# A gated linear attention in front of two MLP blocks: each 128-token unit's attention done in two halves of 64 tokens

## The chip, the core and the metric

The kernel runs on one core of a Trainium2 chip. The metric is device time in microseconds (us) of one execution, taken as the median of several runs. A second source is one execution recorded by the hardware profiler, whose trace gives start and duration of the instructions on each engine: PE (TensorE matmuls), PEld (TensorE weight loads), DVE (VectorE), ACT (ScalarE), POOL (GpSimd), SP (SyncE, which issues the DMAs).

## The reference

```python
# q, k, v, f_logit: (4, 8, 768, 48) float32
f = 1.0 / (1.0 + np.exp(-f_logit))
for t in range(S):
    state = f[:, :, t, :, None] * state + np.einsum('bhd,bhe->bhde', k[:, :, t], v[:, :, t])
    y[:, :, t] = np.einsum('bhd,bhde->bhe', q[:, :, t], state)
x = y as (4, 768, 384)
xn = (x - mean) / np.sqrt(var + 1e-06) * g_ln
x = x + np.maximum(xn @ w_ch1, 0.0) @ w_ch2                      # (384 -> 1536 -> 384)
h = np.maximum(x.transpose(0, 2, 1) @ w_tok1, 0.0) @ w_tok2      # over the 768 tokens, 256 wide
u = x + h.transpose(0, 2, 1)
out = u + np.maximum(u @ w2_ch1, 0.0) @ w2_ch2
```

## The kernel before, in words

**Units.** The tokens are cut into NU = 24 units of C = 128 tokens, one batch each: unit n is chunk c = n // 4 of batch b = n % 4. So units 0 to 3 start from an empty state (c = 0), and units 20 to 23 are the last of their batch (`last`) and need not hand a state on.

**Attention of a unit** (function `attention(n)`). The gates become a running sum along the tokens (`scan`); K is multiplied by exp(sum) (`km`) and Q by exp(-sum) (`qm`), after which the recurrence is a masked product without gates. The 8 heads lie as 4 pairs p, with the two heads r of a pair on partitions 0 to 47 and 64 to 111. The items that run on TensorE are:

- `kp`: 4 transposes of K, evicted by ACT as `kt`;
- `sc`: scores K·Q, for each of 8 heads in two halves of the key tokens, 48 rows by 64 columns of the array, with all 128 query tokens moving. DVE multiplies them with the upper-triangular mask `upper` and writes A (`A0`, `A1`, one for each r);
- `y`: the carried part state·Q (48 rows, only if c > 0), and then the inner part V·A (all 128 rows), summed in the PSUM tiles `yT`;
- `st`: the new part of the state, V·kt (128 rows, 48 moving columns), which `ste` adds to `state[b]` and `std` decays on POOL;
- `yt`: 4 transposes of the result, then `lna`, `lnc` make the layer norm's input, and `tp`: 3 transposes, split by `ah`, `al` into the two parts that the MLP reads.

These are float32 matmuls, and each appears in the trace as two instructions (16 calls of `sc` are 32 instructions).

**MLP.** The weights arrive as 64-bit numbers; `convert` turns each tile of 128x384 into a high and a low float32r part: `.ld` a DMA, `.a`, `.b`, `.c` on DVE, `.h` on ACT, `.l` on DVE or POOL. The first block's MLP takes three units in a step (8 steps); a piece is 9 matmuls of 128x384 (`mm1`, line 492, and `mm2`, line 522). The second block (lines 549, 570, 730, 754) has the same weights' place and follows.

**Order of the work.** Each engine works in the order in which the program emits its instructions. Two mechanisms set it. Up to time slot J = 77 a list written out by hand, `ORDER`, names every item; there `n.sc` is unit n's item, `w3.a` a step of weight tile 3, `m0.4` a piece of MLP step 0, `m0.o20` one of its second product, and `+k` puts k filler matmuls (`busy`, line 439, bf16, 224 columns of zeros, result unused) ahead of the item. After slot 77 the items are sorted by their slot numbers: unit n has s0 = M0 - LEAD + 8(n - 3), its items stand at s0 plus the offset in the table at the end of `attention`, and the MLP puts one piece at every whole slot. `POOL` lists the items that run on GpSimd instead of VectorE; from unit `NV` on, `clamp`, `km` and `qm` all do.

[...]

Of the kernel before, what the change touches and what calls it, by code (L numbers as in the profile page):

```python
# [155 lines left out]
def main_path(ctx, tc, q_t, k_t, f_t, v_n, g_rep, w1, w2, wt1, wt2, w3, w4, out, x1_d, f_d):  # L156
# [11 lines left out]
    upper = const.tile([128, 128], F32, name="upper")  # L168
# [4 lines left out]
    rs = const.tile([128, NU], F32, name="rs")  # L173
    zeros = const.tile([128, 224], BF16, name="zeros")
# [58 lines left out]
    vp = at.enter_context(tc.tile_pool(name="vp", bufs=2))  # L233
# [4 lines left out]
    state = [s1.tile([P2, NP * D], F32, name=f"state{b}") for b in range(B)]  # L238
# [4 lines left out]
    def attention(n):  # L243
# [75 lines left out]

        def scores(z=0):  # L320
            t["sc"] = [scp.tile([128, NP, 128], F32, tag="sc", name="sc") for _ in range(2)]
            busy(t["sc"][0].rearrange("p a c -> p (a c)"), z)
            for p in range(NP):
                for r in range(2):
                    for s in (slice(0, 64), slice(64, 128)):
                        nc.tensor.matmul(t["sc"][r][s, p], t["K"][rows(r), p, s], t["Q"][rows(r), p, :])  # L326

        def scores_e(g):
            a = s2.tile([128, NP, 128], F32, tag=f"A{g}", name=f"A{g}")
            t["A", g] = a  # L330
            nc.vector.tensor_tensor(
                a, t["sc"][g], upper.rearrange("p (o c) -> p o c", o=1).to_broadcast([128, NP, 128]),
                op=ALU.mult)

        def outp(z=0):


            t["yT"] = [atp.tile([128, NP, 128], F32, tag="at", name="yT") for _ in range(2)]
            busy(t["yT"][0].rearrange("p a c -> p (a c)"), z)
            heads = [(p, r, slice(64 * (p % 2), 64 * (p % 2) + (D if p % 2 else 64)))  # L340
                     for p in range(NP) for r in range(2)]
            if c:
# [3 lines left out]
            for p, r, o in sorted(heads, key=lambda x: x[1]):
                h = head(p, r)
                nc.tensor.matmul(t["yT"][r][o, p // 2], t["V"][:, D * h:D * h + o.stop - o.start],  # L348
                                 t["A", r][:, p, :], start=(c == 0 and p < 2), stop=(p > 1))

        def outp_e(r):
            if not r:
                t["ys"] = s1.tile([P2, 2, 2, 128], F32, tag="ys", name="ys")
            nc.scalar.activation(out=t["ys"][:, r], in_=t["yT"][r][:P2, :2], func=AF.Copy)
# [8 lines left out]

        def stat():
            ps = t["st"] = t["yT"][0].rearrange("p a c -> p (a c)")[:, 256:256 + NP * D]
            kt, v = t["kt"], t["V"]
            for p in range(NP):
                for r in range(2):
                    h = head(p, r)
                    w = D if r else 64  # L370
                    nc.tensor.matmul(ps[64 * r:64 * r + w, D * p:D * p + D],  # L371
                                     kt[:, P2 * p + 64 * r:P2 * p + 64 * r + w], v[:, D * h:D * h + D])

        def stat_d():
            s = state[b].rearrange("p (a c) -> p a c", a=NP)
            nc.gpsimd.tensor_tensor(s, s, t["dec"].to_broadcast([P2, NP, D]), op=ALU.mult)

        def stat_e():
            new = t["st"][:P2]
            if c:  # L380
                nc.vector.tensor_tensor(state[b], new, state[b], op=ALU.add)
            else:
                nc.scalar.activation(out=state[b], in_=new, func=AF.Copy)
# [36 lines left out]
        for d, add, f, name in (  # L420
# [12 lines left out]
            if f:  # L433
                add(s0 + d, f, f"{n}.{name}")
# [176 lines left out]
    def start():  # L611
# [11 lines left out]
        for s in state:  # L623
            nc.gpsimd.memset(s, 0.0)
# [429 lines left out]
```

## Time and profile before

| what | value |
|---|---|
| median of 3 runs | 785.78 us (785.74, 785.78, 786.79) |
| span of the profiled execution, first to last instruction | 784.8 us |
| PE busy | 774.3 us, 99% of the span |
| DVE, ACT, POOL busy | 409.8, 325.8, 209.2 us |
| granted TensorE clock | full in all but the last slices |
| chain of work that ended last | PE 92%, DMA 4%, DVE 2% |

The span is 1.0 us below the median of the runs. Busy time of PE is the union of its matmuls, whose recorded durations overlap; how fast matmuls really follow each other is read from the starts of neighbouring groups in the timeline.

### The profile page before, as it was taken

The page shows a single profiled execution, that of the slowest core. Times are in us where ns is not written, and L with a number is a line of the kernel's source. Part 1 is how long each engine was busy: PE and PEld are TensorE (multiplying, and loading weights), DVE is VectorE, ACT ScalarE, POOL GpSimd, SP SyncE. Part 2 cuts the span into 40 slices and gives each one's busy share as a digit, 9 for nine tenths or more (in the row PEclk, how much of TensorE's full clock was granted, in tenths as well). Part 3 has the DMA queues.
Part 4 walks back from the last instruction along what each step waited for, and adds up shares of the span by engine and source line. Part 5 has one row for each costly group of instructions (what it writes and reads, how often), then busy time and mean ns, then how long its engine had stood idle before and what let it go on. Part 6 is the DMA issues. An engine that isn't in the chain of part 4 may idle for free.

```text
span 784.8 us, 14459 instructions
## 1 busy us (share of the span) xinstructions
PE 774.3 (99%) x5785; PEld 727.9 (93%) x5785; DVE 409.8 (52%) x742; ACT 325.8 (42%) x817; POOL 209.2 (27%) x270
## 2 busy tenths in 40 slices
PE   8899999999999999999999999999999999999997
PEld 7799999999999999999999898899899899899886
DVE  6789996564655556554363444434434444344421
ACT  6773552443534435342252544334424344334210
POOL 3642344333433323430014441211111111112000
PEclk9999999999999999999999999999999999999999
DMA  9743553444434445441343632324333342323101
GB/s 252 229 130 107 168 154 101 149 127 156 148 113 142 130 150 153 138 136 51 101 120 95 192 115 84 110 81 132 112 81 91 111 141 74 109 81 104 38 2 44
DMA packets 48604, 93.24 MB, mean 119 GB/s; under 512 B 5520, under 2 KB 26128, under 8 KB 48528
## 3 DMA queue, kind: packets, MB, share of 16 engines
q1 hardware_dynamic: 48528, 92.23, 39.3%
q8 instruction: 47, 0.77, 0.4%
q14 instruction: 29, 0.24, 0.1%
HBM read 76.48 MB, written 15.73 MB: 117 GB/s over the span
## 4 chain that ended last, share of the span: by engine, by line
PE 92%; DMA 4%; DVE 2%; ACT 1%; issue 0%; POOL 0%; SPq 0%; POOLq 0%
PE mo L570 19%; PE mm L549 19%; PE mo L522 19%; PE mm L492 18%; PE rt L730 3%; PE ht L754 3%; PE sc L326 3%; PE yT L348 2%; PE tp L445 2%; DMA firstv<-in_w 1%; PE yT L344 1%; DMA sg<-in_w 1%; PE yT L371 1%; PE y L362 1%; DMA first<-in_k_t 1%; PE kp L310 1%
## 5 line engine op out<-in xcount | busy, mean ns | idle before, releaser
L492 PE MATMUL mm<-xt,w1h 128*128 128x384 f32 x576 | 150.0, 341 | 0.1
L807 POOL TENSOR_TENSOR cs<-cs 128x384 f32<-128x384 f32 x56 | 46.6, 832 | 226.5 <-DVE cs L804 155.9
L492 PEld LDWEIGHTS mm<-xt,w1h 128*128 128x128 f32 x576 | 102.1, 188 | 1.1 <-DVE xt L478 0.3
L522 PE MATMUL mo<-w2h,hh 128*128 128x384 f32 x288 | 100.2, 348 | 0.0
L560 DVE SCALAR_TENSOR_TENSOR hl<-mm,hh 128x512 fp32r<-128x512 f32 x72 | 49.7, 691 | 92.4 <-ACT hh L556 92.4
L570 PE MATMUL mo<-w2h,hh 128*128 128x384 f32 x288 | 97.5, 338 | 0.0
L492 PE MATMUL mm<-xt,w1l 128*128 128x384 f32 x288 | 96.6, 336 | 0.1
L522 PE MATMUL mo<-w2h,hl 128*128 128x384 f32 x288 | 96.6, 335 | 0.0
L570 PE MATMUL mo<-w2h,hl 128*128 128x384 f32 x288 | 96.5, 335 | 0.0
L522 PE MATMUL mo<-w2l,hh 128*128 128x384 f32 x288 | 96.3, 335 | 0.0
L570 PE MATMUL mo<-w2l,hh 128*128 128x384 f32 x288 | 96.3, 334 | 0.0
L556 ACT ACTIVATE hh<-mm 128x512 fp32r<-128x512 f32 x72 | 43.0, 598 | 121.2 <-PE mm L549 121.2
L507 ACT ACTIVATE hh<-mm 128x384 fp32r<-128x384 f32 x96 | 46.9, 489 | 70.0 <-PE mm L492 70.0
L511 DVE SCALAR_TENSOR_TENSOR hl<-mm,hh 128x384 fp32r<-128x384 f32 x96 | 52.9, 554 | 41.5 <-ACT hh L507 41.2
L549 PE MATMUL mm<-xt,w1h 128*128 128x512 f32 x216 | 67.1, 392 | 0.0
L600 DVE TENSOR_TENSOR xr<-mo,xr 128x384 f32<-128x384 f32 x48 | 26.7, 556 | 74.2 <-PE mo L570 74.2
L522 PEld LDWEIGHTS mo<-w2h,hh 128*128 128x128 f32 x288 | 54.1, 188 | 1.3 <-issue 0.9
L570 PEld LDWEIGHTS mo<-w2h,hh 128*128 128x128 f32 x288 | 54.1, 188 | 0.5
L570 PEld LDWEIGHTS mo<-w2l,hh 128*128 128x128 f32 x288 | 54.1, 188 | 0.4
L492 PEld LDWEIGHTS mm<-xt,w1l 128*128 128x128 f32 x288 | 54.1, 188 | 0.4 <-DVE w1l L227 0.4
L522 PEld LDWEIGHTS mo<-w2l,hh 128*128 128x128 f32 x288 | 54.2, 188 | 0.0
L570 PEld LDWEIGHTS mo<-w2h,hl 128*128 128x128 f32 x288 | 54.0, 188 | 0.0
(157 smaller groups left out, 1514.0 us busy)
## 6 DMA issues: line engine op xcount, KB each, us to landing
cs<-in_w SPq DMA_DIRECT2D x48, 384.0 KB, 3.2
sg<-in_w SPq DMA_DIRECT2D x44, 384.0 KB, 3.7
f_d<-cu SPq DMA_DIRECT2D x32, 192.0 KB, 2.0
wf<-f_d SPq DMA_DIRECT2D x32, 192.0 KB, 2.6
F<-in_f_t SPq DMA_DIRECT2D x21, 224.0 KB, 2.8
T<-in_k_t SPq DMA_DIRECT2D x21, 224.0 KB, 2.9
T<-in_q_t SPq DMA_DIRECT2D x21, 224.0 KB, 3.4
x_d<-x SPq DMA_DIRECT2D x24, 192.0 KB, 1.9
```

The source lines that it names most:

```text
L326: nc.tensor.matmul(t["sc"][r][s, p], t["K"][rows(r), p, s], t["Q"][rows(r), p, :])
L492: nc.tensor.matmul(ps, w[:, f, k, :], x[:, k, :], start=(i == 0), stop=(i == 8))
L507: nc.scalar.activation(out=hid(f)[0], in_=t[f], func=AF.Relu)
L511: nc.vector.scalar_tensor_tensor(hl, t[f], 0.0, hh.bitcast(F32), op0=ALU.max, op1=ALU.subtract)
L522: nc.tensor.matmul(ps, x, w[:, f, :], start=(f == lo and i == 0), stop=(f == hi and i == 2))
L549: nc.tensor.matmul(ps, w[:, f, k, :], x[:, k, :], start=(i == 0), stop=(i == 8))
L556: nc.scalar.activation(out=hid(f)[0], in_=t[f], func=AF.Relu)
L560: nc.vector.scalar_tensor_tensor(hl, t[f], 0.0, hh.bitcast(F32), op0=ALU.max, op1=ALU.subtract)
L570: nc.tensor.matmul(ps, x, w[:, f, :], start=(f == lo and i == 0), stop=(f == hi and i == 2))
L600: nc.vector.tensor_tensor(x, ps, x, op=ALU.add)
L730: nc.tensor.matmul(t["r"][j][:, :DM], w[:, s, js], t[x, s], start=(s == 0 and i == 0), stop=(s == NCH - 1 and i == 2))
L807: nc.gpsimd.tensor_tensor(t["u"], t["u"], t["h"], op=ALU.subtract)
```

## The change

The unit's 128 tokens become two halves of HC = 64. Scores are computed only for query and key tokens of the same half, so the half block of the score matrix that the mask set to zero is left out, and the block between the halves is replaced by the state after the first half (`mid`).

- `sc`: the same 16 calls, but 64 moving columns instead of 128; the mask is 64 wide, and `A0`, `A1` have 256 columns instead of 512.
- `st` stands right behind `sc` and gives the state's new part of each half separately: 16 calls of 64 rows instead of 8 of 128. `stm` (new, DVE) makes `mid` = old state + first half's part; `ste` makes the new state from `mid` in a second buffer. Last units need `mid` too, so they now have `kp`, `kt`, the first half of `st`, and `stm`.
- `y` is the carried part of the first half and the inner part for r = 0; `z` (new) is the inner part for r = 1 and the carried part of the second half from `mid`, also in units with c = 0. All use 64 rows and 64 moving columns. Between them stands `yw`: DVE sets one element (`done`) once `y`'s last matmul has ended, and `z`'s first matmul waits for that, since from there on the other half of the array's rows writes a PSUM bank.
- The evictions `yc0`, `yc1` keep their sizes; K's transposes get one buffer for `kt` instead of two, V one more.
- `ORDER`, `POOL`, `A`, LEAD (3 to 7), NV (9 to 12) and the offsets of the slots are new. The initial memsets of `state` go, and two small POOL copies make the narrower mask.

```diff
-P = dict(A=[10, 13, 19, 25, 33, 41, 52, 59, 67], M0=29, LEAD=3, WS=9, ... NV=9, ...)
+P = dict(A=[7, 10, 16, 22, 30, 38, 46, 54, 62], M0=29, LEAD=7, WS=9, ... NV=12, ...)
-POOL: w0.l 3.clamp w1.l 3.km 4.clamp w5.l w12.l w13.l 5.clamp w14.l w16.l w6.l 6.qm w18.l 7.km 8.clamp w20.l
-    w22.l 8.qm 9.clamp 9.qm
+POOL: 3.clamp 0.km 4.clamp 1.km 1.qm 2.km 3.km 3.qm w12.l 5.clamp 4.km 4.qm w1.l w2.l w0.l 6.clamp 5.qm 5.km w4.l
+    w3.l w5.l 6.qm 6.km w13.l w14.l 7.clamp w17.l w15.l 7.qm 9.clamp w18.l 8.km w6.l 8.qm w11.l w7.l 10.clamp w8.l
+    9.qm 9.km 10.qm w19.l w20.l w22.l w21.l w23.l 11.km 11.qm
...
         def scores(z=0):
-            t["sc"] = [scp.tile([128, NP, 128], F32, tag="sc", name="sc") for _ in range(2)]
+            t["sc"] = [scp.tile([128, 512], F32, tag="sc", name="sc") for _ in range(2)]
             for p in range(NP):
                 for r in range(2):
-                    for s in (slice(0, 64), slice(64, 128)):
-                        nc.tensor.matmul(t["sc"][r][s, p], t["K"][rows(r), p, s], t["Q"][rows(r), p, :])
+                    for i in range(2):
+                        nc.tensor.matmul(t["sc"][r][half(i), HC * p:HC * p + HC], t["K"][rows(r), p, half(i)],
+                                         t["Q"][rows(r), p, half(i)])
+        def stat():
+            for p in range(NP):
+                for i in range(1 if last else 2):
+                    for r in range(2):
+                        h, w = head(p, r), width(r)
+                        o = NP * HC + D * p
+                        nc.tensor.matmul(t["sc"][i][64 * r:64 * r + w, o:o + D],
+                                         t["kt"][half(i), P2 * p + 64 * r:P2 * p + 64 * r + w],
+                                         t["V"][half(i), D * h:D * h + D])
+        def stat_m():
+            t["S"] = old(), s1.tile([P2, NP * D], F32, tag="mid", name="mid")
+            if c:
+                nc.vector.tensor_tensor(t["S"][1], new(0), old(), op=ALU.add)
+            else:
+                nc.vector.tensor_copy(t["S"][1], new(0))
+        def carried(i):
+            s = t["S"][1] if i else old()
+            for p in range(NP):
+                for r in range(2):
+                    o = slice(64 * (p % 2), 64 * (p % 2) + width(p % 2))
+                    nc.tensor.matmul(t["yT"][r ^ i][o, r, p // 2], s[rows(r), D * p:D * p + width(p % 2)],
+                                     t["Q"][rows(r), p, half(i)], ...)
+        def inner(r):
+            for p in range(NP):
+                for i in range(2):
+                    h = head(p, r)
+                    o = slice(64 * (p % 2), 64 * (p % 2) + width(p % 2))
+                    nc.tensor.matmul(t["yT"][r ^ i][o, r, p // 2], t["V"][half(i), D * h:D * h + width(p % 2)],
+                                     t["A", r][half(i), p], ...)
         def outp(z=0):
+            t["yT"] = [atp.tile([128, 2, 2, HC], F32, tag="at", name="yT") for _ in range(2)]
             if c:
-                for p, r, o in heads: ... state[b][rows(r), ...], t["Q"][rows(r), p, :]
-            for p, r, o in sorted(heads, key=lambda x: x[1]): ... t["V"][:, ...], t["A", r][:, p, :]
+                carried(0)
+            inner(0)
+            t["half"] = nc.cur_bb.bb.instructions[-1]
+        def outp_w():
+            nc.vector.memset(done, 0.0)
+            t["done"] = nc.cur_bb.bb.instructions[-1]
+            follow(t["done"], t["half"])
+        def outp2():
+            block = nc.cur_bb.bb
+            z = len(block.instructions)
+            inner(1)
+            carried(1)
+            follow(block.instructions[z], t["done"])
...
-                (-8.5, sl.e, pre_km, "km"), (-9, sl.e, pre_tot, "tot"), (-3, sl.p, None if last else ktrans, "kp"),
-                (-2, sl.e, None if last else ktrans_e, "kt"), (-6.1, sl.p, scores, "sc"),
-                (-5, sl.e, ... "A0"), (-5, sl.e, ... "A1"), (2, sl.p, outp, "y"), (3, sl.e, ... "yc0"), (3, sl.e, ... "yc1"),
-                (4, sl.p, outp_t, "yt"), (5, sl.e, ln_a, "lna"), (2, sl.p, None if last else stat, "st"), ...
-                (7, sl.p, trans, "tp"),
+                (-8.5, sl.e, pre_km, "km"), (-9, sl.e, pre_tot, "tot"), (-7, sl.p, ktrans, "kp"),
+                (-6, sl.e, ktrans_e, "kt"), (-4.7, sl.p, scores, "sc"), (-4.7, sl.p, stat, "st"),
+                (-4, sl.e, ... "A0"), (-4, sl.e, ... "A1"), (-3.5, sl.e, stat_m, "stm"), (-3.5, sl.e, ... "ste"),
+                (-2.5, sl.e, ... "std"), (3, sl.p, outp, "y"), (3.05, sl.e, outp_w, "yw"), (3.2, sl.p, outp2, "z"),
+                (4, sl.e, ... "yc0"), (4, sl.e, ... "yc1"), (5, sl.p, outp_t, "yt"), ... (11.1, sl.p, trans, "tp"),
```

The two lists `ORDER` are too long to stand here. These are their items for TensorE alone, in order, the attention's and the fillers (`m` stands for one or more MLP pieces in between):

```
before: 0.kp+17 0.sc 1.kp 0.y+8 0.st 1.sc 0.yt 2.kp+8 0.tp+6 1.y 1.st 2.sc 1.yt 3.kp+4 3.sc 2.y 1.tp 2.st 2.yt+11 4.kp
 4.sc+6 2.tp 3.y 3.st m 3.yt 4.y 4.st m 3.tp 4.yt 5.kp 5.sc 4.tp+4 5.y+6 5.st m 5.yt m+5 5.tp m+10 (m pieces, one +3) 6.kp
 m 6.sc m 7.kp m 6.y 6.st m 6.yt m 8.kp 6.tp 7.sc m 8.sc 7.y m 9.kp m 7.st 9.sc 8.y 8.st m 7.yt m 8.yt m 7.tp m 8.tp m
 10.sc 9.y 9.st m
after: 0.kp+14 0.sc 0.st 0.y+3 1.kp+11 0.z 1.sc 0.yt 1.st 2.kp 1.y 2.sc 0.tp 1.z 2.st 3.kp 2.y 1.yt 2.z 3.sc 3.st 2.yt
 3.y+3 1.tp 3.z 4.kp+3 2.tp 4.sc 3.yt 4.st m 4.y m 4.z m 3.tp 5.kp 5.sc 4.yt 5.st m 5.y m 5.z m 6.kp 6.sc 5.yt m 4.tp
 6.st 5.tp m 6.y m 7.kp m 6.z m 7.sc m 7.st m 6.yt m 7.y m 8.kp 8.sc 7.z m 8.st m 8.y m 7.yt 8.z m 9.kp 9.sc m 9.st m
 8.yt m 9.y 10.kp m 9.z 6.tp 10.sc 8.tp m 10.st 7.tp 9.yt m
```

In the list before, the first weight loads come in the order w5, w0, w14, w15, w13, w4, w3, w1, w2; in the one after, w12, w1, w2, w0, w3, w4, w5, w17, w13, w14.

## Rows read from the trace of the kernel before

**Rows 1.** The profile's page: busy us of each engine (share of the span), instructions.

```profile
PE 774.3 (99%) x5785; PEld 727.9 (93%) x5785; DVE 409.8 (52%) x742; ACT 325.8 (42%) x817; POOL 209.2 (27%) x270
```

**Rows 2.** Waits of TensorE in the whole span: total us, times, longest.

```profile
PE sc L326 <- DVE A L331: 1.7, 1, 1.7
...
PE yT L348 <- DVE A L331: 0.2, 1, 0.2
```

**Rows 3.** Busy us of each engine by stretch (PE, PEld, DVE, ACT, POOL), granted clock, DMA share.

```profile
10.70:35.00 24.30, 21.72 (x373) 18.25 (x373) 19.62 (x33) 17.59 (x45) 13.88 (x18) 1.00 0.92 279
...
10.70:52.70 42.00, 39.28 (x587) 33.99 (x587) 35.72 (x66) 32.08 (x86) 22.21 (x29) 1.00 0.72 214
...
140.70:191.10 50.40, 50.40 (x491) 48.66 (x490) 28.44 (x52) 20.95 (x52) 18.22 (x24) 1.00 0.45 140
```

**Rows 4.** Timeline of TensorE, one unit: start us, us, engine, line, tiles, shapes, count.

```profile
303.69 0.34 PE L492 MATMUL mm<-xt,w1l 128*128 128x384 f32 x1
303.95 1.10 PE L326 MATMUL sc<-T 48*64 48x128 f32 x32
304.88 0.62 PE L344 MATMUL yT<-T,state 48*64 48x128 f32 x16
305.42 1.09 PE L348 MATMUL yT<-A,V 128*64 128x128 f32 x16
306.34 0.62 PE L371 MATMUL yT<-V,kt 128*48 128x48 f32 x16
306.89 0.44 PE L492 MATMUL mm<-xt,w1h 128*128 128x384 f32 x1
...
310.14 0.55 PE L362 MATMUL y<-ident,ys 112*128 112x112 f32 x4
```

**Rows 5.** Timeline of TensorE elsewhere: MLP alone, `sc` alone, `kp`, a last unit.

```profile
65.56 0.33 PE L522 MATMUL mo<-w2h,hh 128*128 128x384 f32 x1
65.73 0.33 PE L522 MATMUL mo<-w2l,hh 128*128 128x384 f32 x1
...
83.23 1.10 PE L326 MATMUL sc<-T 48*64 48x128 f32 x32
84.26 0.44 PE L522 MATMUL mo<-w2h,hh 128*128 128x384 f32 x1
...
295.31 0.55 PE L310 MATMUL kp<-ident,T 112*128 112x112 f32 x4
295.62 0.60 PE L492 MATMUL mm<-xt,w1h 128*128 128x384 f32 x2
...
336.26 1.10 PE L326 MATMUL sc<-T 48*64 48x128 f32 x32
...
338.75 0.44 PE L522 MATMUL mo<-w2h,hh 128*128 128x384 f32 x1
```

**Rows 6.** Timeline of all engines, cut to 303.90 to 303.98 us.

```profile
303.95 0.34 PE L326 MATMUL sc<-T 48*64 48x128 f32 x4
```

**Rows 7.** Timeline of TensorE at the start: fillers (L439) and what followed.

```profile
18.24 0.60 PE L310 MATMUL kp<-ident,first 112*128 112x112 f32 x4 [0.40 <-DVE first L296]
...
27.41 1.21 PE L439 MATMUL y<-zeros 128*128 128x224 bf16 x11 [0.25 <-ACT ys L354]
28.46 0.55 PE L362 MATMUL y<-ident,ys 112*128 112x112 f32 x4
```

**Rows 8.** Groups of DVE and POOL instructions by line, start of the span.

```profile
L331 DVE TENSOR_TENSOR A<-sc,upper 128x512 f32<-128x512 f32 x12 | 8.0, 684 | 0.7 <-PE sc L326 0.7
L299 DVE TENSOR_TENSOR T<-T,eq 112x512 f32<-112x512 f32 x3 | 2.1, 688 | 0.0
L299 POOL TENSOR_TENSOR T<-T,eq 112x512 f32<-112x512 f32 x5 | 8.3, 1662 | 7.3 <-ACT eq L293 7.3
L296 POOL TENSOR_TENSOR T<-T,ek 112x512 f32<-112x512 f32 x5 | 6.6, 1321 | 2.8 <-DMA T<-in_k_t 1.8 <-ACT ek L289 1.0
L227 POOL TENSOR_TENSOR w1l<-cu,w1h 128x384 fp32r<-128x384 f32 x4 | 4.2, 1052 | 3.6 <-ACT w1h L226 3.6
```

More of the change, by code (lines that the diff above doesn't have):

```diff
@@ L173, in main_path @@
     rs = const.tile([128, NU], F32, name="rs")
+    done = const.tile([1, 1], F32, name="done")
     zeros = const.tile([128, 224], BF16, name="zeros")
@@ L237, in main_path @@
     sm = at.enter_context(tc.tile_pool(name="sm", bufs=6))
-    state = [s1.tile([P2, NP * D], F32, name=f"state{b}") for b in range(B)]
+    stp = at.enter_context(tc.tile_pool(name="stp", bufs=2))
+    state = [None] * B
     first = hp.tile([128, 36, 128], F32, tag="hh", name="first")
@@ new lines, in stat_e, with stat_d @@
+        def stat_e():
+            state[b] = stp.tile([P2, NP * D], F32, tag=f"state{b}", name=f"state{b}")
+            nc.vector.tensor_tensor(state[b], new(1), t["S"][1], op=ALU.add)
+        def stat_d():
+            s = state[b].rearrange("p (a c) -> p a c", a=NP)
+            nc.gpsimd.tensor_tensor(s, s, t["dec"].to_broadcast([P2, NP, D]), op=ALU.mult)
+        def carried(i):
[4 more added lines that the diff above has]
+                    nc.tensor.matmul(t["yT"][r ^ i][o, r, p // 2], s[rows(r), D * p:D * p + width(p % 2)],
+                                     t["Q"][rows(r), p, half(i)], start=(i == 0 and p < 2),
+                                     stop=(i == 1 and p > 1))
@@ L335, in outp @@
+        def inner(r):
[4 more added lines that the diff above has]
+                    nc.tensor.matmul(t["yT"][r ^ i][o, r, p // 2], t["V"][half(i), D * h:D * h + width(p % 2)],
+                                     t["A", r][half(i), p], start=(c == 0 and r == 0 and p < 2), stop=False)
         def outp(z=0):
-            t["yT"] = [atp.tile([128, NP, 128], F32, tag="at", name="yT") for _ in range(2)]
@@ L339, in outp @@
-            busy(t["yT"][0].rearrange("p a c -> p (a c)"), z)
-            heads = [(p, r, slice(64 * (p % 2), 64 * (p % 2) + (D if p % 2 else 64)))
-                     for p in range(NP) for r in range(2)]
+            t["yT"] = [atp.tile([128, 2, 2, HC], F32, tag="at", name="yT") for _ in range(2)]
+            busy(t["yT"][0].rearrange("p a g c -> p (a g c)"), z)
             if c:
-                for p, r, o in heads:
-                    nc.tensor.matmul(t["yT"][r][o, p // 2], state[b][rows(r), D * p:D * p + o.stop - o.start],
-                                     t["Q"][rows(r), p, :], start=(p < 2), stop=False)
@@ L346, in outp @@
[L346 to L354, printed above, removed]
+                carried(0)
@@ L362, in outp_t @@
                     nc.tensor.matmul(t["y"][:, i:i + P2], t["ys"][:, r, g], ident[:P2, :P2], is_transpose=True)
[L364 to L383, printed above, removed]
         def ln_a():
```

130 lines of the change are left out of this document (76 added, 54 removed).

## The prediction

> **What bounds the kernel.** I read the page first: TensorE is busy 99% of the span, the other engines 27 to 52% [rows 1]. Busy is not the same as full, so the second view is its waits: 4.5 us in all, five entries [rows 2]. Together they say that after the start TensorE never stands: a microsecond of its stream is a microsecond of the result, and work of other engines counts only if it makes TensorE wait. The third view, busy time by stretch, separates two regimes [rows 3]: from 10.7 to 52.7 us TensorE is short of full while DVE is busy 35.7 of 42 us and the DMA engines 92% of the first 24 us; from 140.7 us TensorE is full for 50.40 us a step (three units) and DVE has 44% free. [...] The fourth view is the timeline of TensorE around one unit [rows 4], where starts of neighbouring groups give what each item takes.
>
> The sum is made against the profiled span, 784.8 us; the median of the runs lies 1.0 us above, and I add that at the end. About 0.2% (1.6 us) is what a measurement of this kernel can tell from none.
>
> **What a unit costs now.** An MLP matmul takes 0.173 us from start to start [rows 5]. From the last MLP matmul to `sc` are 0.26 us, so 0.09 to enter. Then `sc` 0.93, carried part 0.54, inner part 0.92, `st` 0.55; the next 18 MLP matmuls take 3.25 instead of 3.12, so 0.13 after leaving [rows 4]. Sum 3.16 us.
>
> Inside, four small tiles of the array run side by side. Within 0.08 us four matmuls of `sc` have started [rows 6]. I call four such a round. `sc` is 8 rounds, the carried part 4, the inner part 8 rounds of two tiles: (0.92 - 0.05)/8 = 0.109 us for 128 columns, where 0.05 is the first weight load, which nothing hides. `sc` alone, followed by the MLP, takes 1.03 instead of 0.93 [rows 5], so leaving a tile shape costs 0.10 to 0.11. One block of small tiles within MLP work thus costs 0.09 + 0.05 + 0.11 + 0.13 = 0.38 us over its rounds. That is the price of breaking attention into more pieces.
>
> **The price of a half round.** No row shows four tiles with 64 columns. Half of 0.109 is 55 ns. `st` is the nearest: 64-wide weights, 48 columns, 8 rounds in 0.55 less 0.09 to 0.11 for leaving, 55 to 58 ns; its 48 columns would need only 41 at the pace of `sc`, so the weight loads set it there, and a 64-wide load is what the new rounds have too. I take 57, with 55 and 109 (no gain at all from halving) as ends. The state's new part was 8 rounds of two tiles and becomes 8 rounds of four: twice the instructions, same time.
>
> **TensorE's stream after, three kinds of units.**
> - Units 10 to 19, sorted by slots. By the offsets, `sc` and `st` form one block, `y` a second, `z` a third, with an MLP piece between `y` and `z`: 3 x 0.38 + 32 rounds x 0.057 = 2.96, against 3.16. Ten units: -2.0.
> - Hand-ordered part (units 0 to 9, and 10's scores and state). Counting the lists: before, 192 rounds of 0.109, 80 of 0.057, 16 blocks and 10 changes of shape within a block: 20.9 + 4.6 + 6.1 + 1.1 = 32.7, and 0.46 for 10's `st`, which came later: 33.2. After, 320 rounds (units with c = 0 have no carried part in `y`, but now one in `z`) and 35 blocks: 18.2 + 13.3 = 31.5. So -1.7.
> - Last units, 20 to 23. Before, from `sc` to the next MLP matmul 2.49 [rows 5], with 0.09 and 0.13 2.71. After 2.96 (half a `st`, but on two tiles, takes as many rounds), and `kp`, new here: 0.31 [rows 5], with 0.09 after it: 0.40. So +0.65 each, +2.6 in all.
>
> Sum -1.1. The rounds after number 768 against 160 of `st` before, so 55 instead of 57 ns makes it -2.3. Blocks grow from about 30 to 77; 0.04 more or less on each is 1.9 us. So -4 to +2.
>
> **The start.** From the first `kp` on, 71 of the old fillers run, 20 of the new ones, at 1.05/11 = 0.096 us [rows 7]: up to 4.9 us. A filler that stands in front of a wait costs nothing (a `kp` that still waited 0.40 us), one followed at once does (the 11 in front of `yt`) [rows 7]. In the old list about 45 of the 71 are followed at once. 45/71 of 4.9 is 3.1. That TensorE can use the time depends on its suppliers. DVE gives up 5 `km`, 4 `qm`, 3 `.l` and nearly half of twelve `A`s: 9 x 0.69 + 3 x 0.6 + 12 x 0.28 = 11 us [rows 8], and gets `stm`, and `ste` of the first units, back, about 3. POOL takes 5 x 1.32 + 4 x 1.66 + 3 x 1.05 = 16.4 [rows 8], less four memsets of some 0.3: 22.2 becomes about 37.5 of 42 us [rows 3]. DVE's load of 35.7 falls to 28, but the longest load of any supplier hardly changes; it moves to POOL. On the other side w1, w2, w0 are now loaded ahead of tiles that wait, and DMA is what the first 35 us are short of. I take -3. Ends: -8, if nearly all fillers and waits there go, and +6, if POOL's queue holds `km` and `qm` back, behind which `kp`, `sc` and all of a unit stand.
>
> **Edits at no cost.** Narrower `A`s, `stm`, the copies: after 52.7 us DVE's free 44% and ACT's 58% [rows 3] hide them; without that cover, `stm` would cost under half of an `A` (0.68) for each unit. `yw` is a wait put into DVE's queue: behind it stand the MLP's `.l` steps and the weights' conversion, which free the MLP's PSUM banks. DVE meets it when `y` is done or soon after, and `z` comes an MLP piece (9 x 0.173 = 1.56 us) and, by the slots, three transposes later: hidden. Late next, if DVE lags, would be `z`. `kp` from 3 to 7 slots ahead, `tp` from 7 to 11: in slot order K's product stands one and a half slots, some 3 us, ahead of `kp`, and takes POOL 1.32. Units' loads keep their distance to s0. The mask's copies run while the first loads land.
>
> **Sum.** 784.8 - 1.1 - 3 = 780.7; with 1.0 to the median, 781.7.
>
> **Rivals.**
> 1. *The start gains more.* Fillers and waits nearly vanish (DMA order, DVE free): 773 to 778. For: DVE was the releaser of the old waits [rows 2]. Against: POOL's 37.5 of 42.
> 2. *POOL becomes the bound of the start.* `km` and `qm` at 1.32 to 1.66 instead of 0.69; the start gains nothing or loses up to 6: 784.7 to 791. For: the load above, in order behind one queue. It decides once TensorE's idle time from 10.7 to 52.7 us grows by 1.1.
> 3. *The turn from `y` to `z` is not hidden.* A wait that takes the place of none: last matmul's end, DVE, back, some 0.45 us by the tail of a matmul (0.3) and DVE's start; in all 24 units 10.8, so up to 792. For: DVE's queue is full in the start. Against: 44% free later, and an MLP piece in between.
> 4. *Small matmuls do not start faster.* Halving columns does not do what it says, because TensorE takes a new small matmul only so often. `sc` starts 32 in 0.93 us, 29 ns each; `st` 16 in 0.44, 27. If 27.5 is a rate of the engine, 128 instructions a unit take 3.5 instead of 1.82: +1.7 for each of 24, about 822. For: no sustained pace in the trace is faster. Against: four starts at once [rows 6], and that half of 109 and `st`'s rounds both fit loads and columns. It decides from 63 ns a round: 3.7 of gain over 608 more rounds of this kind is 6 ns.
>
> [...]
>
> **Chances.** Forecast, 778 to 784.2: 0.44. Rival 1: 0.11. Rival 2: 0.24, of which 0.13 within 0.2% and 0.11 slower. Rival 3: 0.09, of which 0.02 within 0.2%. Rival 4: 0.12. So faster 0.55, within 0.2% 0.15, slower 0.30. The range 773 to 790 leaves out rival 4 and the top of 2 and 3, about 0.18; the likeliest case's own range is 778 to 784.2.
>
> **What would show it.** Right: `sc` 0.5 and `st` 0.5 us in the timeline, in one block of about 1.1; `y` and `z` 0.6 each up to what follows; a step of 49.8 instead of 50.4 us; no wait of TensorE on `done` after 60 us; `kp` in the last units; about 8 us of fillers and waits between the first `kp` and 53 us instead of 11. Wrong: rounds over 63 ns; waits of TensorE on POOL's K or Q, or on DVE's `done`; DVE idle behind `done` while `.l` steps are due.

## The result: 0.6% slower, and the profile after

The changed kernel takes 791.57 us (median of 11 runs, 790.12 to 793.41), the kernel before 786.15 us (11 runs, 785.14 to 790.27). The ratio is 1.0063, 95% interval 1.0048 to 1.0079. Forecast were 781.7 us and a range of 773 to 790. The profiled execution has a span of 788.9 us, against 784.8.

Line numbers below are those of the changed kernel: `kp` L315, `sc` L338, `st` L350, carried part L386, inner part L395, `yw` L411, `lna` L444, `lnc` (tile `xn`) L454, fillers L500, `ah` L535, MLP products L553 and L583, their `.l` step (tile `hl`) L572, conversions on DVE L208, L213, L218, `km` L301, `qm` L304. (One statement more in e7, e8 and e10 moves the lines from L500 on by one.)

The page's busy line, which answers to [rows 1]:

```profile
PE 768.2 (97%) x6899; PEld 717.1 (91%) x6899; DVE 417.8 (53%) x774; ACT 325.7 (41%) x817; POOL 249.0 (32%) x288
```

TensorE's busy time fell by 6.1 us while the span grew by 4.1. It has less work, and it waits. First the work: the timeline of TensorE for one unit, which answers to [rows 4].

```profile
253.00 0.34 PE L553 MATMUL mm<-xt,w1l 128*128 128x384 f32 x1
253.27 0.45 PE L386 MATMUL yT<-T,state 48*64 48x64 f32 x16
253.54 0.41 PE L395 MATMUL yT<-A,V 64*48 64x64 f32 x16
253.88 0.62 PE L553 MATMUL mm<-xt,w1h 128*128 128x384 f32 x2
...
255.55 0.49 PE L506 MATMUL tp<-ident,xn 128*128 128x128 f32 x3
255.97 0.45 PE L395 MATMUL yT<-A,V 64*64 64x64 f32 x16
256.25 0.41 PE L386 MATMUL yT<-T,mid 48*48 48x64 f32 x16
256.47 0.65 PE L338 MATMUL sc<-T 48*64 48x64 f32 x32
256.94 0.64 PE L350 MATMUL sc<-V,kt 64*48 64x48 f32 x32
```

From the start of `sc` to the start of `st` are 0.47 us for 8 rounds: 58 ns, against 57 forecast. And `z` of one unit, `sc` and `st` of the next stand in a row, without MLP work between: two blocks of small tiles a unit, not three. The waits of TensorE in the whole span (total us, times, longest), which answer to [rows 2]:

```profile
PE sc L338 <- issue: 2.5, 2, 1.6
PE yT L395 <- DVE done L411: 2.4, 2, 2.0
PE mm L553 <- ACT xt L535: 2.3, 1, 2.3
PE mm L553 <- DVE hl L572: 2.3, 3, 0.9
...
PE mo L583 <- DVE hl L572: 0.8, 1, 0.8
```

I cut the span at the first piece of MLP step 2, shortly after the hand-ordered part ends, and at the first piece of step 7:

| stretch | before | after | difference | forecast |
|---|---|---|---|---|
| to step 2 | 140.59 | 145.08 | +4.5 | -4.7 (hand-ordered part -1.7, start -3) |
| steps 2 to 6 | 244.03 | 243.64 | -0.4 | +0.6 (-2.0 and +2.6) |
| rest | 400.2 | 400.2 | 0 | 0 |

The view by stretch for steps 2 to 6, before and after:

```profile
140.59:384.62 244.03, 244.03 (x2251) 235.50 (x2250) 135.40 (x245) 96.96 (x239) 77.07 (x104) 1.00 0.41 128
```

```profile
145.08:388.72 243.64, 241.17 (x2898) 231.12 (x2898) 142.47 (x270) 97.39 (x236) 87.17 (x99) 0.99 0.42 130
```

That the -0.4 of steps 2 to 6 lies near the forecast +0.6 is luck: a gain of 5.4 us and losses of 5.1 us that nobody had forecast stand behind it (e5 below). Three places explain the table.

**The end of the list.** The wait of 2.33 us stands at the first cut. Here is ACT, then TensorE, in their timelines:

```profile
124.32 0.47 ACT L568 ACTIVATE hh<-mm 128x384 fp32r<-128x384 f32 x1
143.84 0.49 ACT L444 ACTIVATE x<-y 128x384 f32<-128x384 f32 x1 [19.05 <-DMA x_d<-x]
...
144.56 0.47 ACT L535 ACTIVATE xt<-tp 128x384 fp32r<-128x384 f32 x1
```

```profile
145.08 1.28 PE L553 MATMUL mm<-xt,w1h 128*128 128x384 f32 x2 [2.33 <-ACT xt L535]
146.16 0.52 PE L553 MATMUL mm<-xt,w1l 128*128 128x384 f32 x1
```

ACT stands 19.05 us before `9.lna`, which needs an `x` buffer. A store frees it: `m0.d0`, which the list names behind `m1.d0`. So SP holds it until step 1's result is there too, at 141.88 us, although unit 0's was complete at 130.9 (DVE's addition of 0.62 us begins at 130.31). Here is SP's row with the five stores:

```profile
141.88 2.31 SPq L653 DMA_DIRECT2D x_d<-x  x5
```

Behind `9.lna` on ACT stands `7.ah`, and step 2's first piece needs that. The matmuls after this wait follow each other at 0.32 us instead of 0.17, and the view by stretch gives a granted clock of 0.50 from 145.5 to 148.8 us; before the fall, TensorE had stood 2.33 us.

**Once a step.** At 167.78, 217.51 and 267.00 us TensorE stands 0.6 to 0.9 us, each time behind `kp`. The timeline of all engines at the first:

```profile
163.74 0.56 DVE L572 SCALAR_TENSOR_TENSOR hl<-mm,hh 128x384 fp32r<-128x384 f32 x1 [0.68 <-ACT hh L568]
...
163.99 1.30 POOL L301 TENSOR_TENSOR T<-T,ek 112x512 f32<-112x512 f32 x1
164.22 1.48 DVE L218 SCALAR_TENSOR_TENSOR cu<-sg,cu 128x384 int32<-128x384 int32 x1
165.24 1.61 POOL L304 TENSOR_TENSOR T<-T,eq 112x512 f32<-112x512 f32 x1
165.62 1.64 DVE L454 SCALAR_TENSOR_TENSOR xn<-x,nm,gln 128x384 f32<-128x384 f32 x1
166.38 0.55 PE L315 MATMUL kp<-ident,T 112*128 112x112 f32 x4
167.18 1.01 DVE L572 SCALAR_TENSOR_TENSOR hl<-mm,hh 128x384 fp32r<-128x384 f32 x2
```

L218 takes 0.55 us elsewhere, `xn` 0.61. Here they last 1.48 and 1.64, and each ends 0.41 us after the POOL product beside which it began. The next `hl` comes 3.4 us after the one before, and the MLP matmul at 167.78 waits for it; `hl` frees a PSUM bank of the MLP. Not every step is caught: of the steps that began while `km` or `qm` ran on POOL between 140 and 340 us, all four `xn` took 1.47 to 1.64 us and the five L208 (0.35 alone) 1.10 to 1.45, but all four `hl` 0.56.

**The start.** The view by stretch (us, then busy us of PE, PEld, DVE, ACT, POOL with counts, granted clock, DMA share, GB/s), which answers to [rows 3]:

```profile
10.70:35.00 24.30, 19.42 (x506) 15.75 (x506) 21.48 (x40) 16.98 (x43) 20.84 (x23) 0.86 0.84 226
35.00:52.70 17.70, 15.60 (x287) 13.38 (x287) 17.25 (x30) 12.05 (x31) 14.81 (x13) 1.00 0.61 197
```

POOL is at 35.65 of 42 us (forecast 37.5). DVE is at 38.73, where 28 was forecast: it gave work away and got busier. The MLP starts at 38.25 us instead of 34.96, and the granted clock was 0.50 from 19.2 to 26.0 us; before it fell, TensorE had stood 1.6 us in the middle of `1.sc`. The longest wait on `done`, 2.0 us at 53.5, is here: L213 in front of `5.yw` took 1.61 us instead of 0.55.

### The profile page after: what moved, and what is told of

The parts are those of the page before. It is cut to its first block, busy times and chain, and to the rows that moved or that the text cites. A ratio compares the mean times of both kernels' runs of the same rounds, so it can differ in the third digit from the quotient of the medians.

```text
span 788.9 us, 16758 instructions
## 1 busy us (share of the span) xinstructions
PE 768.2 (97%) x6899; PEld 717.1 (91%) x6899; DVE 417.8 (53%) x774; ACT 325.7 (41%) x817; POOL 249.0 (32%) x288
## 4 chain that ended last, share of the span: by engine, by line
PE 89%; DVE 6%; DMA 2%; ACT 2%; issue 1%; SPq 0%; DVEq 0%; ACTq 0%
PE mo L583 19%; PE mo L631 19%; PE mm L610 19%; PE mm L553 16%; PE rt L792 3%; PE ht L816 3%; PE tp L506 2%; PE yT L395 2%; PE yT L386 2%; PE sc L338 1%; PE sc L350 1%; PE y L438 1%; DMA sg<-in_w 1%; DVE cu L208 1%; DVE cu L213 1%
## 5 line engine op out<-in xcount | busy, mean ns | idle before, releaser
L553 PE MATMUL mm<-xt,w1h 128*128 128x384 f32 x576 | 152.2, 345 | 4.8 <-ACT xt L535 2.3
L553 PEld LDWEIGHTS mm<-xt,w1h 128*128 128x128 f32 x576 | 102.6, 189 | 7.7 <-DVE hl L572 3.2
L583 PE MATMUL mo<-w2h,hh 128*128 128x384 f32 x288 | 100.9, 350 | 0.8 <-DVE hl L572 0.8
L553 PE MATMUL mm<-xt,w1l 128*128 128x384 f32 x288 | 97.1, 337 | 0.0
L583 PE MATMUL mo<-w2h,hl 128*128 128x384 f32 x288 | 96.6, 335 | 0.0
L583 PE MATMUL mo<-w2l,hh 128*128 128x384 f32 x288 | 96.4, 335 | 0.0
L572 DVE SCALAR_TENSOR_TENSOR hl<-mm,hh 128x384 fp32r<-128x384 f32 x96 | 52.7, 552 | 39.1 <-ACT hh L568 38.5
L583 PEld LDWEIGHTS mo<-w2h,hh 128*128 128x128 f32 x288 | 54.1, 188 | 2.5 <-DVE hl L572 1.1
L553 PEld LDWEIGHTS mm<-xt,w1l 128*128 128x128 f32 x288 | 54.6, 189 | 0.0
L583 PEld LDWEIGHTS mo<-w2l,hh 128*128 128x128 f32 x288 | 54.2, 188 | 0.0
```

The lines of the kernel that those rows point to most:

```text
L553: nc.tensor.matmul(ps, w[:, f, k, :], x[:, k, :], start=(i == 0), stop=(i == 8))
L572: nc.vector.scalar_tensor_tensor(hl, t[f], 0.0, hh.bitcast(F32), op0=ALU.max, op1=ALU.subtract)
L583: nc.tensor.matmul(ps, x, w[:, f, :], start=(f == lo and i == 0), stop=(f == hi and i == 2))
```

## Experiments

The first four ran together (kernel before: 786.85 us, 35 runs), then e5 to e8 (786.61, 17 runs), then e9 and e10 (786.50, 17 runs).

**e1_seam: the stores earlier in the list.**

```diff
-    m0.o23 s1.c m0.r03 m0.r23 m1.o22 m0.o13 7.ah m0.r13 m1.o12 ...
-    m1.r03 10.std m1.d0 m0.d0 m1.o23 m0.d2 m1.d1 m0.d1 10.A1 7.al s3.ld 7.lnr
+    m0.o23 s1.c m0.r03 m0.d0 m0.r23 m0.d2 m1.o22 m0.o13 7.ah m0.r13 m0.d1 m1.o12 ...
+    m1.r03 10.std m1.d0 m1.o23 m1.d1 10.A1 7.al s3.ld 7.lnr
```

> Change kept, but the stores of step 0's rows (m0.d0, m0.d2, m0.d1) stand in SP's queue right behind the work that makes them, and no longer behind m1.d0. Theory: in the changed kernel ACT stood 19.1 us at 9.lna until 143.84 us, for a buffer of x that only the store of unit 0 frees, and that store stood behind one of step 1; TensorE then stood 2.3 us before step 2 and ran 3.4 us at half clock, about 4.3 us lost. Expected: ACT's wait ends some 8 us earlier or more, no wait of TensorE at the seam, the clock full there, 787.3 us. Rival: ACT's late work is not what step 2 waits for, or the conversions take the place: time within 1 us of the changed kernel's.

787.43 us, ratio to before 1.0009 (0.9995 to 1.0024). Moving three of the five stores forward was worth 4.1 us between the two medians. `9.lna` now starts 10.5 us sooner, TensorE has no wait at the cut (step 2 starts at 142.97), and nothing of a half clock shows in that step (49.75 us, the next one 49.73 with the granted clock at 1.00). ACT still stands, for 8.18 us, but nothing that is due is behind it. SP's row with the three stores, then ACT's:

```profile
131.33 5.00 SPq L653 DMA_DIRECT2D x_d<-x  x3
```

```profile
133.35 0.49 ACT L444 ACTIVATE x<-y 128x384 f32<-128x384 f32 x1 [8.18 <-DMA x_d<-x]
```

**e2_kq_late_dve: `km` and `qm` of units 12 to 23 on DVE.**

```diff
-            return nc.gpsimd if n >= P["NV"] or f"{n}.{x}" in POOL else nc.vector
+            return nc.gpsimd if n >= P["NV"] and x == "clamp" or f"{n}.{x}" in POOL else nc.vector
```

> Change kept, but K's and Q's products of units 12 to 23 run on VectorE instead of GpSimd. Theory: a DVE instruction that reads SBUF alone stands until a running GpSimd product ends (xn took 1.64 us beside one, 0.61 else), and this makes the MLP's low part late once a step: waits of TensorE of 1.1, 1.1, 0.9 and 0.3 us behind kp. Expected: those waits go, xn and the conversions go back to 0.6 and 0.55 us, 3 us less, about 788.5 us. Rival (DVE's load decides, not the sharing): 12 x 2 x 0.69 = 16.6 us more on DVE make TensorE wait more, the same time or up to 3 us longer.

Ratio 1.0013 (0.9995 to 1.0030), median 788.39. The stalls behind `kp` are gone, and steps 3 to 5 take 48.70, 48.70 and 48.58 us, against 49.71, 49.49 and 48.83 in the changed kernel. DVE got 24 products more, and TensorE waits less for DVE.

**e3_kq_start_dve: `km` and `qm` of units 0 to 11 on DVE.** The edit takes these 20 names out of the list `POOL`.

> Change kept, but K's and Q's products of units 0 to 11 run on VectorE instead of GpSimd (the order of the items is the same). Theory: between 10.7 and 63 us DVE's conversions and xn took some 12 us more than their shortest, beside GpSimd's products; with fewer of these on GpSimd DVE gets back about 7 us of it and pays 0.69 each, some 10 us for the 14 products of that stretch; K and Q are ready 0.6 to 1 us sooner each. Expected: the MLP starts between 1 us later and 2 us sooner than 38.25 us, time 788 to 792. Rival (the number of DVE's instructions decides): MLP start 4 us or more later and 795 us.

Ratio 1.0031 (1.0014 to 1.0047), median 789.68. The view by stretch from 10.7 to 62.9 us, first the changed kernel, then e3:

```profile
10.70:62.90 52.20, 43.60 (x900) 36.95 (x901) 48.86 (x86) 35.00 (x89) 43.33 (x45) 0.93 0.71 205
```

```profile
10.70:62.90 52.20, 43.92 (x894) 37.13 (x895) 47.49 (x97) 33.99 (x86) 26.81 (x33) 0.90 0.69 204
```

DVE carries out 11 instructions more, at 0.68 us each some 7.5 us, and is busy 1.4 us less. About 9 us (7.5 and 1.4, an estimate) of what counts as DVE's busy time in the changed kernel is thus standing beside POOL. For TensorE it made no difference in this stretch: the MLP starts 1.3 us later, its step 1 begins at the same time (70.50 against 70.27 us), and the waits only have other names, the longest on `done` falling from 2.0 to 0.6. In the two traces only step 2 is shorter by much (50.24 us against 51.71): the wait of 2.3 us at the end of the list is there too, but the granted clock stays at 1.00 behind it. Each trace is one execution; whether e3's others keep the full clock there, and so whether its 1.9 us of median are the edit's, is not shown.

**e4_fillers: fillers put back** (12 ahead of `1.sc`, 4 ahead of `0.yt`, 6 ahead of `2.kp`).

> Change kept, with 22 fillers more (12 ahead of 1.sc, 4 ahead of 0.yt, 6 ahead of 2.kp), 2.1 us of TensorE. Theory: TensorE ran at half clock from 19.2 to 26.0 us after a stretch with waits of 0.7, 1.9 and 0.3 us and few matmuls; fillers fall into these waits. Expected: full clock to the MLP's start, attention items there at half their length, MLP start 1 to 2.5 us sooner, 789 to 790.5 us. Rival: suppliers (DVE, GpSimd) set that stretch and not the clock: full clock, but the MLP starts where it did, and the time is the changed kernel's or up to 1 us longer.

Ratio 1.0062 (1.0042 to 1.0081), as without them. The granted clock stays at 1.00 until 37.4 us (then 0.50 for 3.4 us), the MLP starts 0.8 us sooner, and by step 2 it is 0.3. So the rival holds: with the full clock TensorE reached its waits sooner and then stood (1.27 us ahead of the `kp` at 26.09, 1.62 ahead of the `yt` at 36.30), and the half clock before the MLP's start had cost little. What the half clock behind 37.4 us took back was not separated.

**e5_both: e1 and e2 together.**

> Both earlier edits together: the stores m0.d0, m0.d2, m0.d1 right behind their additions in the list, and km and qm of units 12 to 23 on DVE. Theory (two separate losses: ACT's late start at the seam of list and slots, and the stall once a step while POOL's products hold DVE): the gains add, 791.8 - 4.4 - 3.4 = 784.0 us, no wait at 143 to 147 us, none after kp at 160 to 320, steps of 48.7 us. Rival (one slack: the stalls of a later step only take what an earlier wait leaves, or the half clock of the seam comes back elsewhere): 786 to 787, no better than the better of the two edits by more than 1 us.

784.19 us, ratio 0.9968 (0.9957 to 0.9978): the two losses are separate and add up, and without them the kernel is faster than before. Its steps 2 to 6 take 238.61 us (before: 244.03), a gain of 5.4. To step 2 it takes 143.41 us, still 2.8 more. Its steps 2 to 6 in the view by stretch:

```profile
143.41:382.02 238.61, 238.61 (x2899) 229.13 (x2898) 139.69 (x294) 97.72 (x236) 56.02 (x75) 1.00 0.42 134
```

**e6_split and e7_one_block: the price of a block**, both on top of e5.

```diff
 e6
-                (-4.7, sl.p, stat, "st"),
+                (-3.8 if n >= 12 else -4.7, sl.p, stat, "st"),
 e7
+        one = 0.1 if 12 <= n < 23 else 0
-                (3, sl.p, outp, "y"), (3.05, sl.e, outp_w, "yw"), (3.2, sl.p, outp2, "z"),
+                (3 + one, sl.p, outp, "y"), (3.05 + one, sl.e, outp_w, "yw"), (3.2 + 2 * one, sl.p, outp2, "z"),
```

> As e5_both, but st of units 12 to 23 stands one MLP piece behind sc, where it forms a third block of small tiles within MLP work. Theory (the term of the stream: each block of small tiles costs 0.38 us over its rounds, and the kernel gained more there than forecast because z, sc and st run as one block, so two blocks a unit and not three): 12 x 0.38 = 4.6 us more than e5_both, 788.6, and steps of 49.8 instead of 48.7 us. Rival (a block costs nothing like that, the gain came from faster rounds): within 1.5 us of e5_both.

> As e5_both, but for units 12 to 22 y stands behind its MLP piece, next to the score block of the following unit: the order is y, sc and st of the next unit, z, all one block, and DVE's done is covered by sc and st (1.04 us) instead of an MLP piece (1.56 us). Theory (0.38 us a block, done hidden behind 1 us of small tiles): 11 x 0.38 = 4.2 us less than e5_both, 779.8, steps of 47.6 us. Rival (done not hidden by 1.04 us, because DVE stands in a step of up to 0.65 us and the way there and back takes 0.45): z waits some 0.1 to 0.5 us in each unit, 780.5 to 785.

e6: 788.09 us, ratio 1.0017 (1.0007 to 1.0026), 3.9 us more than e5: 0.33 us a block. In the traces a step takes 49.50 us against 48.71, which is 0.26 a block. e7: 782.57 us, ratio 0.9953 (0.9939 to 0.9967), 1.6 less than e5, where 4.2 had been expected. The timeline of TensorE shows all of a unit as one block:

```profile
203.22 0.45 PE L386 MATMUL yT<-T,state 48*64 48x64 f32 x16
203.49 0.41 PE L395 MATMUL yT<-A,V 64*48 64x64 f32 x16
203.72 0.65 PE L338 MATMUL sc<-T 48*64 48x64 f32 x32
204.18 0.58 PE L350 MATMUL sc<-V,kt 64*48 64x48 f32 x30
204.55 0.26 PE L395 MATMUL yT<-A,V 64*48 64x64 f32 x2
...
204.89 0.41 PE L386 MATMUL yT<-T,mid 48*48 48x64 f32 x14
205.23 0.44 PE L554 MATMUL mm<-xt,w1h 128*128 128x384 f32 x1
```

DVE writes `done` at 204.00, and `z` follows `st` without a gap: a cover of 0.8 us of `sc` and `st` is enough, so that rival is out. Part of what a block gave went back at `kp`, which waits for `km` up to 0.3 us a step, and at one `hl` (0.3).

**e8_best: e7 with the fillers of e4 and `5.yw` ahead of `w13.b`.**

> As e7_one_block, with the fillers of e4_fillers (12 before 1.sc, 4 before 0.yt, 6 before 2.kp) and 5.yw one conversion step earlier in DVE's order, so that 5.z need not wait behind the step of 1.6 us. Theory (z's wait of 2.0 us at 53.5 us is DVE's queue order; the handshake itself is short): 1.5 to 2.5 us less than e7_one_block, z's wait under 0.4 us. Rival (DVE's total work is what is late there, the wait moves to the MLP's hl or to sc): within 1 us of e7_one_block.

783.01 us, ratio 0.9963 (0.9949 to 0.9976): no gain over e7. The longest wait on `done` fell to 0.8 us, and 1.3 us on `cu` (L213) and two waits on `hl`, 1.7 in all, came in its place. The rival holds: in the start it is all of DVE that is late, not one item's place in its queue.

**e9_xn_later: `km` and `qm` stay on POOL, `xn` moves.** As e1, with one offset changed.

```diff
-                ... (7, sl.e, ln_c, "lnc"), ...
+                ... (8.6 if n >= 12 else 7, sl.e, ln_c, "lnc"), ...
```

> As e1_seam, with km and qm of units 12 to 23 still on POOL, but their xn step moved 1.6 slots later in DVE's order, so that it no longer stands in front of the MLP's hl steps when POOL begins km. Theory (DVE's steps that read and write SBUF alone stand while a POOL product runs, and the stall comes from two such steps, 1.47 and 1.44 us instead of 0.61 and 0.35, in a row between two hl): hl is late by one such step at most, the waits of 0.9 us after kp shrink to 0.3 or less, steps of 48.8 to 49.1 instead of 49.7 us, and the time comes to 784.5 to 785.5, 2 to 3 us less than e1_seam, although POOL's and DVE's work is the same. Rival (POOL or DVE has too much work in that part of a step, whatever its order): the wait moves to another step and the time stays at 787 to 788.

785.13 us, ratio 0.9975 (0.9961 to 0.9989), 2.3 us less than e1, with the same instructions on the same engines. In e1, two such steps again stand in a row, `xn` for 1.47 us and then this one:

```profile
211.48 1.44 DVE L208 TENSOR_SCALAR cu<-sg 128x384 int32<-128x384 int32 x1
```

From 192 to 338 us, DVE's groups by line in e1 (count, busy us, mean ns):

```profile
L208 DVE TENSOR_SCALAR cu<-sg 128x384 int32<-128x384 int32 x19 | 10.6, 555 | 0.0
L454 DVE SCALAR_TENSOR_TENSOR xn<-x,nm,gln 128x384 f32<-128x384 f32 x9 | 8.6, 960 | 0.0
```

in e9:

```profile
L208 DVE TENSOR_SCALAR cu<-sg 128x384 int32<-128x384 int32 x19 | 8.9, 468 | 0.0
L454 DVE SCALAR_TENSOR_TENSOR xn<-x,nm,gln 128x384 f32<-128x384 f32 x9 | 7.9, 880 | 0.0
```

and in e5, where POOL has no products:

```profile
L208 DVE TENSOR_SCALAR cu<-sg 128x384 int32<-128x384 int32 x19 | 6.6, 348 | 0.0
L301 DVE TENSOR_TENSOR T<-T,ek 112x512 f32<-112x512 f32 x9 | 6.1, 683 | 0.0
L454 DVE SCALAR_TENSOR_TENSOR xn<-x,nm,gln 128x384 f32<-128x384 f32 x9 | 5.7, 637 | 0.0
```

In e9 DVE still stands beside POOL (468 and 880 ns against 348 and 637 in e5), only where no `hl` is due. What was left is one wait, at 164.14 us, behind unit 10's `xn`, which the edit does not move. So it was not the amount of work that stalled TensorE, but which DVE step met the product.

**e10_km_earlier: e7 with `km` of units 12 to 23 at -9.1 instead of -8.5.**

> As e7_one_block, with km of units 12 to 23 0.6 slots earlier, ahead of xn in DVE's order. Theory (what one block gained, 0.3 us a block, was partly given back by kp, which waits 0.2 to 0.45 us a step for km): no wait of kp from 150 to 340 us, steps of 47.9 to 48.2 us, 0.8 to 1.3 us less than e7_one_block, 781.3 to 781.8. Rival (DVE is late there by then, and the hl step that km is now ahead of becomes the wait): the same time as e7_one_block within 0.4 us, with waits on hl instead of km.

781.94 us, ratio 0.9926 (0.9906 to 0.9946): `kp` no longer waits, and the only wait left from 145 to 380 us is one of 0.3 on `hl`. Against e7's own group the medians differ by 0.6 us, less than expected; the steps are 47.84 to 48.36 us. The view by stretch for steps 2 to 6, e10:

```profile
144.65:380.71 236.06, 235.72 (x2898) 228.84 (x2898) 140.06 (x294) 96.62 (x236) 60.70 (x75) 1.00 0.43 135
```

That is 2.55 us less than e5's 238.61 for 11 blocks fewer, 0.23 a block.

## Why the prediction was wrong, step by step

**The price of a half round: right.** 57 ns were taken, 58 measured; `st` stayed at its old price (0.56 us to what follows, 0.55 before). The 0.05 for a first weight load is what the first matmul of `sc` at 303.95 in the trace before takes over the median one, 0.32 us against 0.27. Rival 4 is out: 32 instructions of `sc` start in 0.47 us, 15 ns each. (Its threshold of 63 ns a round took 3.7 us of gain where the sum has 4.1; 58 is below it either way. The 768 rounds counted for the change are 16 too many, as units with c = 0 have 28 each; that moves nothing.)

**TensorE's stream: right in kind, too pessimistic in size.** The step that failed is "by the offsets, `sc` and `st` form one block, `y` a second, `z` a third". `z` at 3.2 of one unit and `sc` at -4.7 + 8 = 3.3 of the next are neighbours, so they share a block. Two blocks at the forecast's own 0.38 give 2.58 us a unit instead of 2.96, 0.58 less than before; e5's steps 2 to 4 show 1.7 us less for three units, 0.57 each. The last units, forecast at +0.65 each, come to about +0.29 (an estimate): before, step 5 is 1.78 us shorter than step 4 for two units without `kp` and `st`, 0.89 each; in e5 it is 0.10 shorter for three units with half a `st`, 0.03 each; and -0.57 + 0.89 - 0.03 is 0.29. Steps 2 to 6 gain 5.4 us where a loss of 0.6 was forecast. Ten units at -0.57 and four at +0.29 are -4.5 of it. The rest is moved rather than gained: `10.kp`, `10.st` and `9.yt` stand ahead of the cut in the new list and behind it in the old, about 1.3 us (an estimate: the forecast's 0.40 and 0.46, and `9.yt` taken as `kp`, both four transposes of 112x112). The price of a block itself was somewhat high: 0.23 to 0.33 measured (e6, e10).

**"Edits at no cost" failed, and decided the sign.** Two of its sentences were wrong.

- "After 52.7 us DVE's free 44% and ACT's 58% hide them" takes free time as if it lay where it is needed, and POOL's time as if it were separate from DVE's. The 44% is also read from 140.7 us on; from 52.7 to 140.7 us DVE had only 17% free, as the row behind this list shows. DVE's steps that take their operands from SBUF alone stood while a POOL product ran (0.35 became up to 1.45, 0.61 up to 1.64), while `hl`, which reads PSUM, kept its 0.56. DVE had 36% free in step 4 (246.5 to 296.0 us), yet two such steps between two `hl` stopped TensorE. e2 took the products away and e9 only moved `xn`; both removed the stall. It cost 3.1 us. `xn` and L218 read two tiles from SBUF, L208 one, and `hl` one beside its PSUM tile; what holds the first three and not `hl`, no run here separates.
- "Units' loads keep their distance to s0" looked at what is loaded, not at what is stored. Nothing in the forecast followed SP's order at the end of the list, where a store behind another step's store holds an `x` buffer, ACT behind that, and TensorE behind ACT. It cost 4.1 us between the medians (e1), the half clock included.

The stretch from 52.7 to 140.7 us in the kernel before (DVE is the third busy time):

```profile
52.70:140.70 88.00, 87.80 (x788) 84.02 (x789) 73.20 (x131) 39.76 (x89) 35.73 (x46) 1.00 0.44 133
```

**Up to step 2: -4.7 forecast (the start -3, the hand-ordered part -1.7), +2.8 measured without the wait at the end of the list (e5).** The fillers did go: 2.6 us of them in e5 against 7.9. But TensorE's time without a matmul, from the first `kp` to step 2, grew from 2.9 us (129.89 less 126.97 busy) to 8.3 (132.48 less 124.21), as much as the fillers gave. "DVE's load of 35.7 falls to 28" is the step: it rose to 38.7, and e3 shows most of why: some 9 us of DVE's busy time from 10.7 to 62.9 us are standing beside what moved to POOL. Rival 2's own sign came: TensorE's idle time from 10.7 to 52.7 us grew by 4.3 (2.72 to 6.98), where 1.1 was to decide. Its mechanism, POOL's queue, did not: TensorE waits on POOL itself for only 0.7 us in `kp`, and with the products back on DVE (e3) the MLP starts no sooner; that only exchanged one DVE load for another. That DVE is what is late there is read from the waits and from the chain of work that ended last, of which DVE's three conversion lines make up 29% from 10 to 60 us (before, 1.9% for L214); no run made DVE's work in the start less, so it is argued and not shown. Fillers (e4) and the place of `5.yw` (e8) changed nothing measurable. Up to 1.3 us of the 2.8 are the three items that moved ahead of the cut. How the rest divides among DVE's load, the order of the weights and the half clock (e5's granted clock is 0.98 from 38.28 us to step 2, and 0.993 over its whole span) was not separated and stays open. Of the two parts, the loss lies ahead of the MLP's start, 38.28 us in e5 against 34.96; from there to step 2 the rows are, before and in e5:

```profile
34.96:140.59 105.63, 105.29 (x1005) 99.69 (x1004) 89.24 (x164) 54.13 (x129) 44.06 (x56) 1.00 0.44 132
```

```profile
38.28:143.41 105.13, 102.77 (x1270) 95.53 (x1267) 85.76 (x160) 52.21 (x129) 63.94 (x76) 0.98 0.42 130
```

**The turn from `y` to `z` (rival 3): hidden, as forecast.** After 62 us no run shows a wait on `done`, and e7 shows it hidden behind 0.8 us; there `done` is written 0.10 us after `y`'s last matmul ends in the trace. No run leaves the wait out, so whether `z` needs it is not shown. In the start of the changed kernel it cost 2.4 us, in two waits, where DVE was late.

**Sum, by the spans of the traces.** Before to e5: +2.8 up to step 2 and -5.4 in steps 2 to 6, together -2.6. From e5 to the changed kernel 6.7 us come back: 1.7 up to step 2 and 2.0 within it (51.71 us against 49.75 in e1) at the end of the list, and 3.1 by the stalls (1.0 in step 2, 49.75 against 48.74, and 2.1 in steps 3 to 6). That makes the +4.1 of the profiled executions.

## What to carry to other kernels

Work moved from DVE to POOL was not free for DVE here: some 9 us of its 48.9 in the start (an estimate, e3) were standing beside it. Look which DVE steps run while POOL's product does, and which of them stand in front of a step that frees PSUM. In a list ordered by hand, follow every queue to the end of the list, the stores too, since here a store behind another one held a buffer, and with it ACT for 19.05 us and TensorE for 2.33. Before breaking work into more blocks, place the pieces so that neighbours share a block: here it was worth 0.2 to 0.3 us each, and e10, with one block a unit, no stall and the stores in order, is 0.7% faster than the kernel before.

## What the runs showed of the hardware that was not expected

- In the changed kernel, from 140 to 340 us, the DVE steps with operands from SBUF alone that began beside `km` or `qm` on POOL ended 0.2 to 0.4 us after that product, however short they are by themselves: L208 needs 0.35 us and took up to 1.45. In the start more of DVE's busy time was standing (about 9 of 48.9 us, an estimate) than the products moved to POOL cost on DVE (7.5).
- Four small tiles side by side (48 rows by 64 columns, 64 moving columns) kept a pace of 15 ns per matmul instruction over 32 instructions; entering and leaving such a block cost 0.23 to 0.33 us (e10, e6).
- Behind the wait of 2.33 us the granted clock was 0.50 for 3.4 us in the changed kernel, and in e3, with a wait of 2.3 us at the same place, 1.00 (145.3 to 149.0 us); waits of 0.6 to 0.9 us amid full MLP work (167.78, 217.51, 267.00) left it at 1.00.
